# Two groups of value matmuls in one job with one accumulation, and the q score matmuls without a pause, in an attention and MoE kernel

## The chip, the cores and the metric

The kernel runs on one core of one Trainium2 chip. The metric is the device time of one execution in microseconds, as the median of several runs. TensorE (PE) does the matmuls, and its weight loads (PEld) are listed apart; VectorE is DVE, ScalarE is ACT, GpSimd is POOL, and SyncE (SP) issues the DMAs.

## The reference

For each of four batches, 49 agent rows attend to 12480 keys, and 12480 queries attend to the 49 agents; the result goes through a dense layer with the gate `h - tanh(h)`.

```python
def _attn_ref(q, k, v, agents):
    scale = 1.0 / np.sqrt(q.shape[-1])
    def sm(a, b):
        s = scale * (a @ b.transpose(0, 2, 1))
        s = s - s.max(-1, keepdims=True)
        e = np.exp(s)
        return e / (e.sum(-1, keepdims=True) + 1e-09)
    a2k = sm(agents, k)
    agent_v = a2k @ v
    q2a = sm(q, agents)
    return (q2a @ agent_v).astype(np.float32)

def _moe_ref(x, w_in, w_out):
    h = x @ w_in
    g = h - np.tanh(h)
    return (g @ w_out).astype(np.float32)
```

B = 4, N = 12480, C = 128, 49 agents, 2048 hidden units, all float32.

## The kernel before, in words

**The main work.** The 4 x 12480 query rows are cut into 104 blocks of 480 (26 to a batch), and each block has 8 steps of two 128-wide chunks of the hidden layer. `m1` (L441, L442) issues four matmuls of 480 columns into `h`, of which PSUM has three buffers. `act` makes `y` (tanh, L451) and `z` (square, L453) on ACT and `g = h*z` on DVE (L455). POOL copies `g` to `gh` in the rounded format (L485), DVE makes the rest `gl = g - gh` (L490), and `m2` issues six matmuls of 480 columns into the block's accumulator `misc` (L502 and L503 wait for `gh`, L504 for `gl`). The last step of every second block has no split and uses two plain float32 matmuls instead (L500). `finish` takes the accumulator to `o` (L617), and a DMA writes it out. All PSUM tiles named `misc` share two buffers, and the block's accumulator holds one of them from its first `m2` to `finish`.

**The work beside it.** For each pair of blocks `q_softmax` makes the scores of 960 queries (eight float32 matmuls, L396), the maxima, `qe` (POOL, L409) and the probabilities `pp` (POOL, L421); `q_transpose` turns them (L428). While batch b runs its main work, `phase1(b+1)` prepares the agents' attention of the next batch as 34 jobs: 13 `scores` (L238), two for the maximum, 13 `av`, one `sums`, four of `project`, and one empty place. A job is a generator: it goes on by one `yield` in each step of the main loop. Three jobs are started in each pair of blocks, at the steps that `KS` names.

**The value jobs.** The 98 tiles of 128 keys are in 13 groups of 8 (the last has 2). `av(g)` in batches 1 to 3 asks for the load of `v` two groups ahead (four buffers `v0` to `v3`), subtracts the maximum into a tile `ke` on POOL (L276; `ke` has two buffers), takes the exponential on ACT (L278), and issues eight float32 matmuls of 129 columns into a fresh `misc` tile (L292). Tiles of even number write 64 partitions and those of odd number the 49 partitions above them. DVE then copies (first group, L320) or adds (L322) the 113 x 129 result to `acc` in SBUF. Batch 0 has its own first phase, before the main loop, with one accumulation over all groups.

**What sets the order.** The kernel is written step by step, but a scheduler arranges the instructions of each engine when the program is built, so the order on an engine is not that of the code. On the chip each engine then takes its instructions in that fixed order.

Of the kernel before, what the change touches and what calls it, by code (L numbers as in the profile page):

```python
# [11 lines left out]
F32 = mybir.dt.float32  # L12
# [63 lines left out]
class Build:  # L76
# [84 lines left out]
    def phase1(self, b):  # L161
# [108 lines left out]
        def av(g):  # L270
            vt = ahead("v", load_v, g, vb - 1 if b else 1)
            n = tiles(g)
            sv = st["s"][:, g * GT * A : (g * GT + n) * A].rearrange("p (t a) -> p t a", a=A)
            e3 = sv if b == 0 else self.small.tile([128, GT, A], F32, tag="ke", name="ke")[:, :n]
            eng = nc.vector if b == 0 else nc.gpsimd
            eng.tensor_tensor(e3, sv, st["mb"][:, None, :].broadcast_to([128, n, A]), ALU.subtract)  # L276
# [3 lines left out]
            if b == 0:  # L280
                if g == 0:
                    st["ps"] = self.ph.tile([128, 2, 512], F32, tag="h", name="h")[:, 0, :]
                ps, first, last = st["ps"], g == 0, g == NG - 1
            else:
                ps, first, last = self.misc(), True, True
            flat = e3.rearrange("p t a -> p (t a)")
            width = C if b == 0 else C + 1
            for t in range(n):
# [4 lines left out]
                    ps[HALF * odd : HALF * odd + w, :width],  # L293
                    flat[:r, t * A : t * A + w],
                    vt[:r, t, :width],
# [4 lines left out]
            if b == 0:  # L300
                if g == 0:
                    st["es"] = self.small.tile([128, GT * A], F32, tag="ke", name="es")
                elif g < NG - 1:
                    e0 = st["s"][:, : GT * A] if g == 1 else st["es"]
                    nc.vector.tensor_tensor(st["es"], e0, flat, ALU.add)
                if g == NG - 2:
                    st["em"] = self.small.tile([128, A], F32, tag="m", name="es")
                    nc.vector.tensor_reduce(
                        st["em"], st["es"].rearrange("p (t a) -> p a t", a=A), axis=AX.X, op=ALU.add
                    )  # L310
                if g < NG - 1:
                    return
                es = st["em"]
                col = ps[:A, C : C + 1]
                for i, (lhs, r) in enumerate(((es, 128), (e3[:, 0, :], 128), (e3[:, 1, :], TAIL))):
                    nc.tensor.matmul(col, lhs[:r], self.ones[:r, :1], start=(i == 0), stop=(i == 2))
                return
# [422 lines left out]
```

## Time and profile before

| | us |
|---|---|
| median of 3 runs | 2182.68 (2182.53 to 2185.22) |
| profiled execution, its own time | 2180.92 |
| its span | 2179.1 |
| PE busy in the span | 2144.5 (98%) |
| weight loads (PEld) busy | 1799.3 (83%) |
| DVE busy | 2026.2 (93%) |
| ACT busy | 1813.1 (83%) |
| POOL busy | 1395.5 (64%) |

The mean granted TensorE clock of the run is 0.992, and it is 1.00 in all stretches after the first 100 us. A matmul's record is longer than the distance to the next one's start, since matmuls are pipelined; so a pause of PE is seen as idle time only where it is longer than the overlap. The distance between starts shows how fast PE goes. The value jobs of batches 1, 2 and 3 lie in the stretches 296 to 504, 832 to 1041 and 1368 to 1577 us.

### The profile page before, as it was taken

The page shows a single profiled execution, that of the slowest core. Times are in us where ns is not written, and L with a number is a line of the kernel's source. Part 1 is how long each engine was busy: PE and PEld are TensorE (multiplying, and loading weights), DVE is VectorE, ACT ScalarE, POOL GpSimd, SP SyncE. Part 2 cuts the span into 40 slices and gives each one's busy share as a digit, 9 for nine tenths or more (in the row PEclk, how much of TensorE's full clock was granted, in tenths as well). Part 3 has the DMA queues.
Part 4 walks back from the last instruction along what each step waited for, and adds up shares of the span by engine and source line. Part 5 has one row for each costly group of instructions (what it writes and reads, how often), then busy time and mean ns, then how long its engine had stood idle before and what let it go on. Part 6 is the DMA issues. An engine that isn't in the chain of part 4 may idle for free.

```text
span 2179.1 us, 31204 instructions
## 1 busy us (share of the span) xinstructions
PE 2144.5 (98%) x11089; PEld 1799.3 (83%) x11089; DVE 2026.2 (93%) x2120; ACT 1813.1 (83%) x2179; POOL 1395.5 (64%) x933
## 2 busy tenths in 40 slices
PE   7899999999999999999999999999999999999998
PEld 7688878888888887888888888888888888888887
DVE  7898999999999999889999999998999999999998
ACT  4688888888888788888898878888889898989987
POOL 1356567666666556667666556667667677676766
PEclk9799999999999999999999999999999999999999
DMA  9211111110011111111101110121100101010000
GB/s 353 86 58 60 56 38 57 59 57 28 28 48 57 59 48 46 58 59 48 37 19 57 57 50 19 56 65 33 36 20 19 37 19 37 19 37 19 28 10 20
DMA packets 65906, 108.75 MB, mean 50 GB/s; under 512 B 4048, under 2 KB 44240, under 8 KB 65744
## 3 DMA queue, kind: packets, MB, share of 16 engines
q1 hardware_dynamic: 65744, 106.68, 15.2%
q8 instruction: 91, 1.49, 0.3%
q14 instruction: 71, 0.58, 0.1%
HBM read 81.10 MB, written 25.56 MB: 49 GB/s over the span
## 4 chain that ended last, share of the span: by engine, by line
PE 88%; DVE 6%; POOL 3%; issue 2%; ACT 0%; DMA 0%; POOLq 0%; SPq 0%; DVEq 0%; ACTq 0%
PE h L441 15%; PE h L442 15%; PE misc L504 15%; PE misc L502 14%; PE misc L503 14%; PE misc L500 4%; PE misc L396 4%; PE misc L238 3%; POOL gh L485 2%; DVE gl L490 2%; DVE g L455 2%; PE misc L292 2%; PE misc L428 1%; PE h L212 1%; PE misc L370 0%
## 5 line engine op out<-in xcount | busy, mean ns | idle before, releaser
L485 POOL TENSOR_SCALAR gh<-g 128x960 fp32r<-128x960 f32 x780 | 1207.3, 1549 | 665.0 <-DVE g L455 416.5
L490 DVE TENSOR_TENSOR gl<-g,gh 128x960 fp32r<-128x960 f32 x780 | 977.4, 1254 | 89.8 <-PE misc L504 55.7
L455 DVE TENSOR_TENSOR g<-h,z 128x960 f32<-128x960 f32 x832 | 950.5, 1146 | 30.5 <-ACT z L453 27.3
L451 ACT ACTIVATE y<-h 128x960 f32<-128x960 f32 x832 | 802.9, 970 | 186.2 <-PE h L442 182.1
L453 ACT ACTIVATE z<-y 128x960 f32<-128x960 f32 x832 | 832.4, 1007 | 24.3 <-DVE g L455 7.2
L441 PE MATMUL h<-pT,awh 98*128 98x480 f32 x1664 | 662.0, 398 | 1.9 <-DVE awl L374 1.4
L442 PE MATMUL h<-pT,awl 98*128 98x480 f32 x1664 | 631.7, 380 | 0.3 <-DVE awl L374 0.3
L504 PE MATMUL misc<-gl,wo_h 128*128 128x480 f32 x1560 | 607.6, 390 | 3.0 <-DVE gl L490 2.9
L502 PE MATMUL misc<-gh,wo_l 128*128 128x480 f32 x1560 | 601.8, 386 | 4.9 <-POOL gh L485 4.9
L503 PE MATMUL misc<-gh,wo_h 128*128 128x480 f32 x1560 | 593.9, 381 | 0.0
L441 PEld LDWEIGHTS h<-pT,awh 98*128 98x128 f32 x1664 | 313.5, 188 | 65.9 <-issue 13.2
L442 PEld LDWEIGHTS h<-pT,awl 98*128 98x128 f32 x1664 | 315.2, 189 | 57.5 <-issue 10.5
L502 PEld LDWEIGHTS misc<-gh,wo_l 128*128 128x128 f32 x1560 | 294.4, 189 | 59.9 <-POOL gh L485 15.7
L504 PEld LDWEIGHTS misc<-gl,wo_h 128*128 128x128 f32 x1560 | 292.6, 188 | 56.4 <-DVE gl L490 7.9
L503 PEld LDWEIGHTS misc<-gh,wo_h 128*128 128x128 f32 x1560 | 293.3, 188 | 47.1 <-issue 1.2
L409 POOL TENSOR_TENSOR qe<-qe,qm 120x392 f32<-120x392 f32 x52 | 74.2, 1426 | 63.7 <-ACT qe L407 63.7
L396 PEld LDWEIGHTS misc<-ag,qt 128*120 128x120 f32 x832 | 96.3, 186 | 4.0 <-issue 0.3
L617 ACT ACTIVATE o<-misc 128x480 f32<-128x480 f32 x104 | 58.7, 564 | 48.7 <-PE misc L500 33.6
L396 PE MATMUL misc<-ag,qt 128*120 128x49 f32 x832 | 93.6, 265 | 0.0
L500 PE MATMUL misc<-g,wo_f 128*128 128x480 f32 x208 | 92.9, 569 | 0.0
L421 POOL TENSOR_TENSOR pp<-qe,pp 120x392 fp32r<-120x392 f32 x52 | 69.4, 1335 | 36.6 <-ACT pp L419 36.4
L238 PEld LDWEIGHTS misc<-ag,kt 128*128 128x128 f32 x588 | 72.1, 191 | 2.5
(92 smaller groups left out, 864.0 us busy)
## 6 DMA issues: line engine op xcount, KB each, us to landing
qt<-qT SPq DMA_DIRECT2D x52, 480.0 KB, 3.4
outT<-o SPq DMA_DIRECT2D x52, 480.0 KB, 2.6
kt<-kT SPq DMA_DIRECT2D x48, 512.0 KB, 3.6
v<-v SPq DMA_DIRECT2D x36, 512.0 KB, 4.1
vt<-v SPq DMA_DIRECT2D x12, 512.0 KB, 9.4
raw<-w_in SPq DMA_DIRECT2D x4, 512.0 KB, 9.1
raw<-w_out SPq DMA_DIRECT2D x4, 512.0 KB, 8.9
kt<-kT SPq DMA_DIRECT2D x4, 128.0 KB, 2.1
```

What stands on the lines that cost most here:

```text
L396: nc.tensor.matmul(ps[:TT, t * A : (t + 1) * A], qt[:, t * TT : (t + 1) * TT], self.ag[:, b, :], start=True, stop=True)
L441: nc.tensor.matmul(h[:, c, :BLK], aw[0][:A2, sl], pT[:A2], start=True, stop=False)
L442: nc.tensor.matmul(h[:, c, :BLK], aw[1][:A2, sl], pT[:A2], start=False, stop=True)
L451: nc.scalar.activation(y, h[:, :, :BLK], AF.Tanh, scale=TSC)
L453: nc.scalar.activation(z, y.rearrange("p c n -> p (c n)"), AF.Square)
L455: nc.vector.tensor_tensor(self.pair(g), h[:, :, :BLK], self.pair(z), ALU.mult)
L485: self.nc.gpsimd.tensor_scalar(gh, g, 1.0, 0.0, ALU.mult, ALU.add)
L490: self.nc.vector.tensor_tensor(gl, g, gh.bitcast(F32), ALU.subtract)
L500: nc.tensor.matmul(acc[:, :BLK], self.wo_f[:, c, :], gh[:, x], start=first, stop=last)
L502: nc.tensor.matmul(acc[:, :BLK], self.wo_l[:, f, :], gh[:, x], start=first, stop=False)
L503: nc.tensor.matmul(acc[:, :BLK], self.wo_h[:, f, :], gh[:, x], start=False, stop=False)
L504: nc.tensor.matmul(acc[:, :BLK], self.wo_h[:, f, :], gl[:, x], start=False, stop=last)
```

## The change

In batches 1 to 3 the 13 jobs `av(g)` become 7 jobs `av_two(j)`. Such a job asks for the loads of both groups, subtracts for the first group, yields, subtracts for the second, yields, issues both exponentials, yields, and issues up to 16 matmuls into one `misc` tile with one accumulation; then it makes one copy or add. `ke` still has two buffers, and a job fills both. A batch's 34 jobs become 28. In `q_softmax` the eight score matmuls, which had a `yield` after the fourth and after the eighth, are followed by both yields. The value code of batch 0 is the same as before.

```diff
+        def av_two(j):
+            gs = [g for g in (2 * j, 2 * j + 1) if g < NG]
+            vts = [ahead("v", load_v, g, vb - 1) for g in gs]
+            es = []
+            for g in gs:
+                n = tiles(g)
+                sv = st["s"][:, g * GT * A : (g * GT + n) * A].rearrange("p (t a) -> p t a", a=A)
+                e3 = self.small.tile([128, GT, A], F32, tag="ke", name="ke")[:, :n]
+                mb = st["mb"][:, None, :].broadcast_to([128, n, A])
+                nc.gpsimd.tensor_tensor(e3, sv, mb, ALU.subtract)
+                es.append(e3)
+                yield
+            for e3 in es:
+                nc.scalar.activation(e3, e3, AF.Exp, scale=SCALE)
+            yield
+            ps = self.misc()
+            todo = [(g, t, e3, vt) for g, e3, vt in zip(gs, es, vts) for t in range(tiles(g))]
+            for x, (g, t, e3, vt) in enumerate(todo):
...
+                nc.tensor.matmul(
+                    ps[HALF * odd : HALF * odd + w, : C + 1],
...
+                    start=x < 2,
+                    stop=x >= len(todo) - 2,
+                )
+            yield
             acc = st["acc"][: HALF + A]
-            if g == 0:
+            if j == 0:
                 nc.vector.tensor_copy(acc, ps[: HALF + A, : C + 1])
             else:
                 nc.vector.tensor_tensor(acc, acc, ps[: HALF + A, : C + 1], ALU.add)
...
-        jobs += [av(g) for g in range(NG)] + [sums()]
+        jobs += [av(g) for g in range(NG)] if b == 0 else [av_two(j) for j in range(-(-NG // 2))]
+        jobs += [sums()]
...
-            if t % 4 == 3:
-                yield
+        yield
+        yield
```

**The order on PE.** The first value job of batch 1, from the eighth matmul of its first group on; `v0` and `v1` are the groups' values. Before:

```order
L292 MATMUL misc_2908<-v0_87,ke_2875 49x129
L504 MATMUL misc_2742<-gl_2825,wo_h_84 128x480
L502 MATMUL misc_2742<-gh_2797,wo_l_85 128x480
L503 MATMUL misc_2742<-gh_2797,wo_h_84 128x480
L504 MATMUL misc_2742<-gl_2825,wo_h_84 128x480
L502 MATMUL misc_2742<-gh_2823,wo_l_85 128x480
L503 MATMUL misc_2742<-gh_2823,wo_h_84 128x480
L441 MATMUL h_2901<-pT_2759,awh_590 128x480
L442 MATMUL h_2901<-pT_2759,awl_591 128x480
L441 MATMUL h_2901<-pT_2759,awh_590 128x480
L442 MATMUL h_2901<-pT_2759,awl_591 128x480
L504 MATMUL misc_2742<-gl_2847,wo_h_84 128x480
```

And of the change (L331 was L292, L526 was L504, L524 was L502, L525 was L503, L463 and L464 were L441 and L442), from the ninth value matmul on:

```order
L331 MATMUL misc_2931<-v1_88,ke_2886 64x129
L526 MATMUL misc_2742<-gl_2825,wo_h_84 128x480
L524 MATMUL misc_2742<-gh_2797,wo_l_85 128x480
L525 MATMUL misc_2742<-gh_2797,wo_h_84 128x480
L526 MATMUL misc_2742<-gl_2825,wo_h_84 128x480
L524 MATMUL misc_2742<-gh_2823,wo_l_85 128x480
L525 MATMUL misc_2742<-gh_2823,wo_h_84 128x480
L463 MATMUL h_2902<-pT_2759,awh_590 128x480
L464 MATMUL h_2902<-pT_2759,awl_591 128x480
L463 MATMUL h_2902<-pT_2759,awh_590 128x480
L464 MATMUL h_2902<-pT_2759,awl_591 128x480
L331 MATMUL misc_2931<-v1_88,ke_2886 49x129
```

The second group's matmuls follow at once, but not in one run: the first job's 16 stand as runs of 9, 4, 1 and 2 with matmuls of the main work between them. The value matmuls of a batch stood in runs of 8, 8, 8, 7, 1, 8, 8, 8, 8, 8, 7, 1, 8, 8, 2 and now stand in runs of 9, 4, 1, 2, 10, 1, 5, 16, 4, 12, 9, 4, 3, 16, 2: 15 runs to a batch both times. The eight score matmuls of a pair (L396) stand in one run in all pairs but the first, before as after.

**The order on POOL.** In the middle of batch 1's value jobs, beginning with a `gh` copy; `ke` is the subtraction of a value job, `pp` that of the query softmax. Before:

```order
L485 TENSOR_SCALAR gh_3258<-g_3256 128x960
L276 TENSOR_TENSOR ke_3412<-s_740,mb_2663 128x392
L485 TENSOR_SCALAR gh_3307<-g_3305 128x960
L485 TENSOR_SCALAR gh_3337<-g_3335 128x960
L421 TENSOR_TENSOR pp_3320<-qe_3226,pp_3320 120x8x49
L276 TENSOR_TENSOR ke_3569<-s_740,mb_2663 128x392
L485 TENSOR_SCALAR gh_3358<-g_3356 128x960
L485 TENSOR_SCALAR gh_3380<-g_3378 128x960
L485 TENSOR_SCALAR gh_3401<-g_3399 128x960
L276 TENSOR_TENSOR ke_3704<-s_740,mb_2663 128x392
```

And of the change (L507 was L485, L319 was L276, L443 was L421):

```order
L507 TENSOR_SCALAR gh_3294<-g_3292 128x960
L319 TENSOR_TENSOR ke_3326<-s_744,mb_2663 128x392
L319 TENSOR_TENSOR ke_3337<-s_744,mb_2663 128x392
L443 TENSOR_TENSOR pp_3358<-qe_3261,pp_3358 120x8x49
L507 TENSOR_SCALAR gh_3345<-g_3343 128x960
L319 TENSOR_TENSOR ke_3461<-s_744,mb_2663 128x392
L507 TENSOR_SCALAR gh_3368<-g_3366 128x960
L319 TENSOR_TENSOR ke_3468<-s_744,mb_2663 128x392
L507 TENSOR_SCALAR gh_3405<-g_3403 128x960
L507 TENSOR_SCALAR gh_3428<-g_3426 128x960
```

The four subtractions of two jobs and a `pp` now stand beside three `gh` copies, where two or three copies stood between one subtraction and the next. The same piece stands in each of batches 1, 2 and 3. Ahead of a batch's value jobs (but for one score matmul in the first step of the main loop) and from the next batch's first score job on, PE's order is the same as before.

## Rows read from the trace of the kernel before

**Rows 1.** The page: busy time of each engine, and the chain that ended last.

```profile
PE 2144.5 (98%) x11089; PEld 1799.3 (83%) x11089; DVE 2026.2 (93%) x2120; ACT 1813.1 (83%) x2179; POOL 1395.5 (64%) x933
PE 88%; DVE 6%; POOL 3%; issue 2%; ACT 0%; DMA 0%; POOLq 0%; SPq 0%; DVEq 0%; ACTq 0%
```

**Rows 2.** Windows: length, busy us (instructions) of PE, PEld, DVE, ACT, POOL, clock, DMA, GB/s.

```profile
296.00:504.00 208.00, 207.74 (x1125) 171.05 (x1123) 190.92 (x202) 174.89 (x210) 143.94 (x98) 1.00 0.18 55
832.00:1041.00 209.00, 208.76 (x1132) 172.05 (x1131) 192.46 (x203) 175.02 (x210) 144.86 (x98) 1.00 0.18 55
1368.00:1577.00 209.00, 208.77 (x1131) 172.03 (x1130) 192.54 (x203) 175.44 (x211) 143.60 (x98) 1.00 0.14 45
1650.00:2150.00 500.00, 500.00 (x2417) 423.21 (x2416) 481.98 (x479) 449.39 (x519) 359.63 (x227) 1.00 0.08 25
```

**Rows 3.** Timeline of PE about one value job of eight matmuls: start, us, what.

```profile
471.41 0.38 PE L442 MATMUL h<-pT,awl 98*128 98x480 f32 x1
471.72 1.09 PE L292 MATMUL misc<-v,ke 128*64 128x129 f32 x16
472.75 0.48 PE L504 MATMUL misc<-gl,wo_h 128*128 128x480 f32 x1
473.07 0.38 PE L502 MATMUL misc<-gh,wo_l 128*128 128x480 f32 x1
473.29 0.38 PE L503 MATMUL misc<-gh,wo_h 128*128 128x480 f32 x1
```

**Rows 4.** Timeline of PE about a run of one value matmul.

```profile
435.14 0.37 PE L504 MATMUL misc<-gl,wo_h 128*128 128x480 f32 x1
435.44 0.42 PE L292 MATMUL misc<-v,ke 128*49 128x129 f32 x2
435.80 1.07 PE L500 MATMUL misc<-g,wo_f 128*128 128x480 f32 x2
```

**Rows 5.** Chain that ended last, two of its pieces in the last batch.

```profile
1956.80 1.62 PE misc L396 x16
...
1968.08 1.61 PE misc L500 x4
```

**Rows 6.** Groups by line: shapes xcount | busy us, mean ns | idle before, releasers.

```profile
L485 POOL TENSOR_SCALAR gh<-g 128x960 fp32r<-128x960 f32 x780 | 1207.3, 1549 | 665.0 <-DVE g L455 416.5 <-PE misc L503 72.3 <-DVE qs L415 65.0
...
L455 DVE TENSOR_TENSOR g<-h,z 128x960 f32<-128x960 f32 x832 | 950.5, 1146 | 30.5 <-ACT z L453 27.3
L453 ACT ACTIVATE z<-y 128x960 f32<-128x960 f32 x832 | 832.4, 1007 | 24.3 <-DVE g L455 7.2
L451 ACT ACTIVATE y<-h 128x960 f32<-128x960 f32 x832 | 802.9, 970 | 186.2 <-PE h L442 182.1
...
L421 POOL TENSOR_TENSOR pp<-qe,pp 120x392 fp32r<-120x392 f32 x52 | 69.4, 1335 | 36.6 <-ACT pp L419 36.4
...
L276 POOL TENSOR_TENSOR ke<-s,mb 128x392 f32<-128x392 f32 (+1 forms) x39 | 48.2, 1240 | 9.5 <-PE misc L292 9.5
...
L322 DVE TENSOR_TENSOR acc<-acc,misc 113x129 f32<-113x129 f32 x36 | 10.1, 280 | 3.0 <-PE misc L292 3.0
```

**Rows 7.** Timeline of POOL where batch 1's first two subtractions stand together.

```profile
282.10 2.80 POOL L276 TENSOR_TENSOR ke<-s,mb 128x392 f32<-128x392 f32 x2
284.87 1.96 POOL L485 TENSOR_SCALAR gh<-g 128x960 fp32r<-128x960 f32 x2
289.08 1.74 POOL L485 TENSOR_SCALAR gh<-g 128x960 fp32r<-128x960 f32 x1 [2.25 <-PE misc L504]
```

**Rows 8.** Timeline of PE in the same stretch, the rows with a wait.

```profile
285.92 0.48 PE L502 MATMUL misc<-gh,wo_l 128*128 128x480 f32 x1 [0.65 <-POOL gh L485]
287.89 0.48 PE L504 MATMUL misc<-gl,wo_h 128*128 128x480 f32 x1 [0.39 <-DVE gl L490]
290.87 0.48 PE L502 MATMUL misc<-gh,wo_l 128*128 128x480 f32 x1 [0.53 <-POOL gh L485]
```

**Rows 9.** The page's DMA issues: what, queue, count, KB each, us to landing.

```profile
v<-v SPq DMA_DIRECT2D x36, 512.0 KB, 4.1
```

More of the change, by code (lines that the diff above doesn't have):

```diff
@@ L270, in av @@
         def av(g):
-            vt = ahead("v", load_v, g, vb - 1 if b else 1)
+            vt = ahead("v", load_v, g, 1)
             n = tiles(g)
[L273 to L276, printed above, removed]
+            e3 = st["s"][:, g * GT * A : (g * GT + n) * A].rearrange("p (t a) -> p t a", a=A)
+            nc.vector.tensor_tensor(e3, e3, st["mb"][:, None, :].broadcast_to([128, n, A]), ALU.subtract)
             yield
@@ L279, in av @@
             yield
-            if b == 0:
-                if g == 0:
[L282 to L285, printed above, removed]
+            if g == 0:
+                st["ps"] = self.ph.tile([128, 2, 512], F32, tag="h", name="h")[:, 0, :]
+            ps, first, last = st["ps"], g == 0, g == NG - 1
             flat = e3.rearrange("p t a -> p (t a)")
-            width = C if b == 0 else C + 1
             for t in range(n):
@@ L292, in av @@
                 nc.tensor.matmul(
-                    ps[HALF * odd : HALF * odd + w, :width],
+                    ps[HALF * odd : HALF * odd + w, :C],
                     flat[:r, t * A : t * A + w],
-                    vt[:r, t, :width],
+                    vt[:r, t, :C],
                     start=(first and t < 2),
@@ L299, in av @@
             yield
[L300 to L316, printed above, removed]
-                return
+            if g == 0:
+                st["es"] = self.small.tile([128, GT * A], F32, tag="ke", name="es")
+            elif g < NG - 1:
+                e0 = st["s"][:, : GT * A] if g == 1 else st["es"]
+                nc.vector.tensor_tensor(st["es"], e0, flat, ALU.add)
@@ new lines, in av @@
+            if g == NG - 2:
+                st["em"] = self.small.tile([128, A], F32, tag="m", name="es")
+                nc.vector.tensor_reduce(
+                    st["em"], st["es"].rearrange("p (t a) -> p a t", a=A), axis=AX.X, op=ALU.add
+                )
+            if g < NG - 1:
+                return
+            col = ps[:A, C : C + 1]
+            for i, (lhs, r) in enumerate(((st["em"], 128), (e3[:, 0, :], 128), (e3[:, 1, :], TAIL))):
+                nc.tensor.matmul(col, lhs[:r], self.ones[:r, :1], start=(i == 0), stop=(i == 2))
@@ new lines, in av_two @@
+        def av_two(j):
[16 more added lines that the diff above has]
+            for x, (g, t, e3, vt) in enumerate(todo):
+                r = rows(g, t)
+                odd = t % 2
+                w = A if odd else HALF
+                nc.tensor.matmul(
+                    ps[HALF * odd : HALF * odd + w, : C + 1],
+                    e3.rearrange("p t a -> p (t a)")[:r, t * A : t * A + w],
+                    vt[:r, t, : C + 1],
+                    start=x < 2,
+                    stop=x >= len(todo) - 2,
+                )
+            yield
@@ L318, in av @@
             acc = st["acc"][: HALF + A]
-            if g == 0:
+            if j == 0:
                 nc.vector.tensor_copy(acc, ps[: HALF + A, : C + 1])
```

## The prediction, made before the changed kernel ran

> **What bounds the kernel now.** I read the page first. PE is busy for 98% of the span and carries 88% of the chain that ended last; DVE is busy for 93% and the weight loads for 83% [rows 1]. The reader is to see that two engines are near the limit, so the averages alone don't tell which of them sets the time. The windows do. In the three stretches with value jobs PE is idle for 208 - 207.74 = 0.26, 209 - 208.76 = 0.24 and 209 - 208.77 = 0.23 us, and in the last 500 us for nothing, while DVE has 16 to 18 us to spare in each [rows 2]. So PE is the bound there, and the pauses that a change could remove are 0.73 us in all, plus what is hidden under PE's overlapping records. Next I read the timeline for PE's pace: two 480-column matmuls start 0.22 us apart (473.07 to 473.29) [rows 3]. The kernel's time is then the sum of what PE issues, plus the places where it stands still, and I cost the change by these two.
>
> **What the value matmuls cost PE.** Eight of them in one run: from the start of the matmul before (471.41) to that of the second one behind (473.07) are 1.66 us, where the two ordinary distances are 0.44; the run costs 1.22 us [rows 3]. The distance just behind the first is 472.75 to 473.07, or 0.32 and not 0.22, so 0.10 of this falls after the run. A run of one costs 435.80 - 435.14 - 0.22 = 0.44 us [rows 4], and with the same 0.10 behind it 0.54. I take it that matmuls go in pairs of even and odd tiles (they write different partitions) and that a lone one costs as much as a pair. Then three more pairs cost 1.22 - 0.54 = 0.68, or about 0.22 a pair, and a run has a fixed part of 0.54 - 0.22 = 0.32 to 1.22 - 4 x 0.22 = 0.34 us; I use 0.34.
>
> **What the change does to that sum.** In the built order a batch has 15 runs before and 15 now, so the fixed parts stay: 45 x 0.34 us both times. A run of odd length fills its last pair by half. Before, a batch's runs hold 51 pairs, now 52 (9, 4, 1, 2 are 5 + 2 + 1 + 1, and so on). This adds 3 x 0.22 = **+0.66 us**. Merging the jobs therefore brings PE nothing, since the scheduler cut the 16 into pieces.
>
> **The score matmuls.** They stood in one run already: the chain shows all 16 of their records (two to a float32 matmul) as one piece of 1.62 us [rows 5]. In the built order this holds before and after for every pair but the first. The cost is **0**.
>
> **The adds.** 18 of the 36 adds on DVE go: 18 x 0.280 = 5.0 us of DVE time [rows 6]. In the value stretches DVE has 16 us to spare each and PE hardly waits [rows 2], so I count **0** on the path. If DVE were the bound, it would be the whole 5.0 (a rival, below).
>
> **The exponentials, the subtractions and the loads** stay in number. The loads of `v` are asked for two at a time; they land in a median of 4.1 us [rows 9], and a group is used one job, about five steps of ten 0.22-us matmuls or 11 us, after its load was asked for. What waits behind such a load on SP's queue is a query load or an output, and the 11 us cover these too: **0**. Without that cover a late load would hold PE for up to 4.1 us.
>
> **The subtractions' places on POOL.** This is the term that no row prices. `ke` has two buffers, and a job now fills both, so the next job's subtraction waits on POOL until PE is through with the value matmuls that read the buffer; the `gh` copies are queued behind it, and PE's L502 waits for these. I bound it at the densest place, the piece of POOL's order in the section on the change. In the built order, between PE's first use of `gh_3345` and that of `gh_3405` PE has 20 ordinary matmuls and four short transposes (about 0.3 us): 20 x 0.22 + 0.3 = 4.7 us. POOL has two subtractions and two copies to do in that time. Two subtractions in a row took 2.80, two copies in a row 1.96, one copy beside DVE work 1.74 us [rows 7]. At best this is 2.80 + 1.96 = 4.8 us, just PE's pace. At worst every subtraction is as long as the longer of the two must have been (2.80 - 0.98 = 1.82, with a copy's 0.98 for the other) and every copy 1.74: 2 x 1.82 + 2 x 1.74 = 7.1 us, 2.4 too long. Against this stands what POOL has in hand when the piece begins. From the end of `h_3328` (the tile from which `gh_3345` is made) to the first use of `gh_3345` PE has 22 matmuls (4.8), the plain pair (1.61 [rows 5]), a run of 4 (0.34 + 0.44) and one of 12 (0.34 + 1.32): 8.9 us. The chain it needs is y 0.97, z 1.01, g 1.15 and gh 1.55 [rows 6], 4.7 us; two subtractions and `pp` (2.80 + 1.34) ahead of the copy would fill the rest if none of it overlapped, and most does, since they need not wait for `h_3328`. So the cost is between 0 and 2.4 us a batch. A gain is no end of it, because PE's idle time in a whole value stretch is 0.26 us at most. I take 0.5, nearer to the lower end as the best case just fits and the slack at the start is real: **+1.5 us** for three batches, with ends of -0.7 (every present pause gone) and +7.2.
>
> **The sum.** 0.66 + 0 + 0 + 0 + 1.5 = +2.2 us on the profiled execution's own 2180.92 us, which is 1.8 below the median of the runs shown; I put it on that median: 2182.7 + 2.2 = **2184.9 us**. A difference of 0.2%, 4.4 us, is about what a measurement of this kernel can tell from no change, so I forecast no change.
>
> **Rivals.**
> - *Slower: the second subtraction holds POOL's queue.* The trace has one place where two subtractions stand together, at the start of each batch's value jobs; there two copies come behind them and PE waits 0.65 + 0.39 + 0.53 = 1.57 us [rows 7, 8]. The change keeps that place and makes a denser one. If it costs the upper end, 2.4 us in each of three batches, the time is 2182.7 + 0.7 + 7.2 = 2190.6. It decides against my forecast from (4.4 - 0.7) / 3 = 1.2 us a batch on. Against it: at the place in the trace no value matmuls gave PE other work, and here 16 lie ahead. A sentence apart: the Trainium skill, SBUF — State Buffer, Who interferes with whom, says that a DVE instruction with two SBUF inputs contends with a GpSimd one that reads SBUF; the copies' 0.98 alone and 1.74 beside DVE [rows 7] agree, and by it the lengths near the worst case are the likely ones wherever `gl` runs beside. Chance 0.20.
> - *Slower: the accumulator waits for the tile.* A value tile is now open over up to four steps, and the next block's accumulator needs its buffer. Each late opening would cost what may stand ahead of the add on DVE, one 1.15-us operation [rows 6], and the add's 0.28: 1.4 us, once a batch, +4.3 with the 0.7: 2187.7. In the built order two `m1` (1.8 us) stand between the first tile's last matmul and that opening, which covers it. Chance 0.05.
> - *Faster: DVE is the bound after all.* DVE is busy for 482 of the last 500 us [rows 2]. If every removed add counted, the time would be 2182.7 - 5.0 = 2177.7. Against it: the adds lie where DVE has room, and their rows name no PE that waits. The Trainium skill's Perfetto Trace Analysis, Identifying the Most-Contended Engine, would judge PE by its weight loads and not by its matmul rows; by that, PE's 83% is under DVE's 93% [rows 1] and this rival is what follows. The pace of 0.22 us without a pause speaks against it here. Chance 0.07.
> - *Faster: the change does what its words say,* and the 16 go through PE in one run. Seven runs a batch instead of 15 save 24 x 0.34 = 8.2, and 49 pairs instead of 51 save 6 x 0.22 = 1.3: 2173.2 us. The built order excludes it, unless the fixed part belongs to the job and not to the run; the run of one that costs 0.54 speaks against that. Chance 0.02.
>
> **How the numbers follow.** My forecast has 0.66. Faster by over 0.2%: 0.07 + 0.02 = 0.09. Slower by over 0.2%: 0.20 + 0.05 = 0.25. Within: 0.66. The range goes from 2178.0, at the edge of the DVE rival, to 2191.0, just over the upper end of the POOL rival; it leaves out about a tenth. The forecast's own range is 2181 to 2187.
>
> **What would show it.** Right: 15 runs of L331 a batch at 0.34 us plus 0.22 a pair, 18 adds of 0.28 us, PE idle for under 1.5 us in each value stretch, and DVE's busy time lower by 5 us with the span unchanged. The POOL rival: L524 waits for `gh` at the middle of the value jobs in every batch, with a subtraction of 1.8 us or a wait for PE just ahead on POOL. The DVE rival: the stretch ends earlier by as much as DVE lost. Wrong in another way: value runs whose cost doesn't follow the pairs, or pauses of PE outside the value stretches.

## The result: slower by 0.17%, within the forecast, one reason of it wrong

The changed kernel takes **2187.93 us** (median of 22 runs, 2182.51 to 2190.89), the kernel before 2184.32 beside it (22 runs, 2180.41 to 2186.46). The ratio is 1.0017, 95% interval 1.0011 to 1.0024: 2.4 to 5.2 us more. The forecast was 2184.9 us, the range 2178.0 to 2191.0.

The page of the changed kernel, busy time and chain (lines behind the value jobs stand 22 lower than before: the `gh` copy is L507, the matmul that waits for it L524; the value matmuls are L331):

```profile
PE 2149.4 (98%) x11089; PEld 1803.5 (82%) x11089; DVE 2024.7 (93%) x2102; ACT 1810.3 (83%) x2179; POOL 1384.6 (63%) x933
PE 89%; DVE 6%; POOL 3%; issue 2%; ACT 0%; DMA 0%; POOLq 0%; SPq 0%; DVEq 0%; ACTq 0%
```

PE's share of the chain is 89% instead of 88% [rows 1], DVE has 18 instructions fewer, and PE is still the bound. DVE's busy time fell by 1.5 us only and not by the 5 of the adds, since its `gl` operations took 3 us longer in all (977.4 before, 980.5 now). The windows of the three value stretches and of the end are those of [rows 2], each moved along with its stretch:

```profile
300.00:508.00 208.00, 207.18 (x1103) 168.54 (x1102) 190.67 (x200) 172.04 (x209) 135.71 (x96) 1.00 0.18 53
837.00:1046.00 209.00, 208.16 (x1107) 169.44 (x1106) 191.60 (x201) 173.04 (x210) 136.69 (x97) 1.00 0.17 53
1374.00:1583.00 209.00, 208.19 (x1108) 169.48 (x1107) 191.70 (x202) 172.96 (x211) 137.61 (x97) 1.00 0.14 43
1657.00:2157.00 500.00, 500.00 (x2417) 423.47 (x2416) 482.27 (x479) 448.94 (x518) 358.75 (x227) 1.00 0.07 25
```

PE is now idle for 0.81 to 0.84 us in each stretch instead of 0.23 to 0.26; the last 500 us are as they were.

**Where the profiled difference lies.** The profiled executions differ by 7.4 us (spans 2179.1 and 2186.5), twice the medians' 3.6. I set the end of each output piece on ScalarE against the same piece of before. 4.29 us are there by 270 us, before the first value job of the change; then 0.93, 1.47 and 0.80 us come in the three batches, and nothing elsewhere. (Of these, 0.16 to 0.25 us a batch come behind the last value job, where the jobs that follow stand at other places; in batch 1 that is 559 to 680 us.) So the change costs 3.2 us, and the 4.29 are no part of it. They go with the granted clock in the first 90 us. Two windows of before, then the same two of the change:

```profile
57.00:70.00 13.00, 9.85 (x24) 4.86 (x23) 10.47 (x24) 3.37 (x8) 0.00 (x0) 0.50 0.57 180
...
73.00:87.00 14.00, 12.75 (x58) 10.27 (x59) 12.37 (x14) 9.21 (x13) 7.17 (x6) 0.83 0.12 36
```

```profile
57.00:70.00 13.00, 10.12 (x25) 5.11 (x25) 10.16 (x25) 2.99 (x7) 0.00 (x0) 0.51 0.58 186
...
73.00:87.00 14.00, 12.37 (x37) 9.81 (x38) 9.61 (x12) 6.06 (x8) 5.79 (x4) 0.51 0.01 1
```

The figure behind POOL's count is the granted clock. In 73 to 87 us the change ran at half speed (0.51, the level of 1.2 GHz) and PE has 37 records, before ran at 0.83 and has 58. Across the profiles below the difference that stands at 270 us is -0.9 to +5.8 us, in no order that goes with the edits. All later readings are therefore steps between two outputs, not differences of spans: "start" is what stood at 270 us, "batch" what each batch's value jobs added to the profile of before.

**The value runs.** A whole job of 16 in one run, and a run of three, in PE's timeline (start, us, what):

```profile
351.00 0.38 PE L525 MATMUL misc<-gh,wo_h 128*128 128x480 f32 x1
351.31 1.98 PE L331 MATMUL misc<-v,ke 128*64 128x129 f32 x32
353.22 0.48 PE L526 MATMUL misc<-gl,wo_h 128*128 128x480 f32 x1
353.54 0.38 PE L524 MATMUL misc<-gh,wo_l 128*128 128x480 f32 x1
...
374.54 0.38 PE L526 MATMUL misc<-gl,wo_h 128*128 128x480 f32 x1
374.85 0.64 PE L331 MATMUL misc<-v,ke 128*49 128x129 f32 x6
375.42 0.48 PE L463 MATMUL h<-pT,awh 98*128 98x480 f32 x1
375.75 0.38 PE L464 MATMUL h<-pT,awl 98*128 98x480 f32 x1
```

Read as in [rows 3], from the start ahead to the start of the second behind, less two ordinary distances, the 16 cost 353.54 - 351.00 - 0.44 = 2.10 us and the three 375.75 - 374.54 - 0.44 = 0.77. By 0.34 a run and 0.22 a pair it would be 2.10 and 0.78. All runs of a batch together cost 16.93 us before and 16.99 now; 0.18 of each run that stands beside the plain pair belongs to that pair (two runs before, one now), which leaves 16.57 and 16.81. The batch's last run, of two matmuls, does not follow the prices: it costs 0.91 us and not 0.56, before as now.

**The score matmuls, the adds and the rest.** In the chain that ended last, the 16 score records are one piece as in [rows 5]; the adds are 18 at the old length [rows 6]; POOL's subtractions have the old length and more idle time ahead of them (14.1 us instead of 9.5):

```profile
391.50 1.62 PE misc L418 x16
```

```profile
L507 POOL TENSOR_SCALAR gh<-g 128x960 fp32r<-128x960 f32 x780 | 1189.1, 1526 | 669.3 <-DVE g L477 444.4 <-PE misc L525 77.4 <-PE misc L526 44.9
...
L319 POOL TENSOR_TENSOR ke<-s,mb 128x392 f32<-128x392 f32 (+1 forms) x39 | 48.2, 1242 | 14.1 <-PE misc L331 6.6 <-ACT y L473 5.3 <-ACT z L475 1.4
L343 DVE TENSOR_TENSOR acc<-acc,misc 113x129 f32<-113x129 f32 x18 | 5.0, 277 | 0.0
```

**The waits.** In batch 1 PE waits three times in the middle of the value jobs, for `gh`: 0.48 us at 385.23, 0.15 at 426.59, 0.19 at 467.19. Before, it waited 0.26 at 331.38 and 0.24 at 537.37. Batches 2 and 3 repeat this. By the distances of the starts (a record hides part of a wait) the three are 1.30 us too long, the two of before 0.82: +0.48 (with the 0.10 us that each also leaves behind it, as in [rows 3], it is +0.58). The longest, on PE and on POOL:

```profile
383.17 0.48 PE L524 MATMUL misc<-gh,wo_l 128*128 128x480 f32 x1
...
385.23 0.48 PE L524 MATMUL misc<-gh,wo_l 128*128 128x480 f32 x1 [0.48 <-POOL gh L507]
```

```profile
372.58 0.95 POOL L319 TENSOR_TENSOR ke<-s,mb 128x392 f32<-128x392 f32 x1 [1.76 <-ACT y L473]
373.50 1.96 POOL L507 TENSOR_SCALAR gh<-g 128x960 fp32r<-128x960 f32 x2
375.64 1.63 POOL L319 TENSOR_TENSOR ke<-s,mb 128x392 f32<-128x392 f32 x1 [0.19 <-PE misc L331]
377.25 1.90 POOL L507 TENSOR_SCALAR gh<-g 128x960 fp32r<-128x960 f32 x1
382.12 3.06 POOL L507 TENSOR_SCALAR gh<-g 128x960 fp32r<-128x960 f32 x2 [2.96 <-PE misc L525]
```

A subtraction that waited for value matmuls (375.64) does stand ahead. But POOL is idle for 2.96 us between the copy behind it and the two copies that PE waits for. The row puts the end of this down to PE's L525. That is only the matmul that ended last: in the built order (as e_ke4_fixed below writes it out) it reads the tile copied at 377.25, and the last reader of the buffer that the copy at 382.12 fills is the L525 that started at 379.02. What the copy starts with is its own `g`: 606 of this trace's 780 copies start 0.15 to 0.19 us after their `g` has ended on DVE, and so do these two. PE, DVE and the second copy there:

```profile
379.23 0.38 PE L526 MATMUL misc<-gl,wo_h 128*128 128x480 f32 x1
```

```profile
379.70 1.16 DVE L512 TENSOR_TENSOR gl<-g,gh 128x960 fp32r<-128x960 f32 x1 [1.41 <-POOL gh L507]
380.78 2.22 DVE L477 TENSOR_TENSOR g<-h,z 128x960 f32<-128x960 f32 x2
383.15 1.16 DVE L512 TENSOR_TENSOR gl<-g,gh 128x960 fp32r<-128x960 f32 x1 [0.15 <-POOL gh L507]
```

```profile
383.18 2.00 POOL L507 TENSOR_SCALAR gh<-g 128x960 fp32r<-128x960 f32 x1
```

DVE takes a `gl` and the two `g` back to back. The `gl` needs the copy that ended at 379.16 and one of two `gl` buffers, and by the built order the last reader of its buffer is the L526 at 379.23. It starts 0.09 us after that matmul has ended, and in batches 2 and 3 it is the same (0.09 us behind the L526 that ended at 917.32 and at 1454.50). So the wait goes back to PE itself, which reads a `gl` tile late, over three operations on DVE, to the copies. The second copy then takes 2.00 us and the first 1.00, as DVE's next `gl` began 0.03 us ahead of the second (last section). That speaks against the subtraction already; the experiments decide it.

### The profile page after: what moved, and what is told of

Its sections match the earlier page's. It is cut to its first block, busy times and chain, and to the rows that moved or that the text cites. A ratio compares the mean times of both kernels' runs of the same rounds, so it can differ in the third digit from the quotient of the medians.

```text
span 2186.5 us, 31233 instructions
## 1 busy us (share of the span) xinstructions
PE 2149.4 (98%) x11089; PEld 1803.5 (82%) x11089; DVE 2024.7 (93%) x2102; ACT 1810.3 (83%) x2179; POOL 1384.6 (63%) x933
## 4 chain that ended last, share of the span: by engine, by line
PE 89%; DVE 6%; POOL 3%; issue 2%; ACT 0%; DMA 0%; POOLq 0%; SPq 0%; DVEq 0%; ACTq 0%
PE h L463 15%; PE h L464 15%; PE misc L526 15%; PE misc L524 15%; PE misc L525 14%; PE misc L418 4%; PE misc L522 4%; PE misc L238 3%; POOL gh L507 2%; DVE g L477 2%; PE misc L331 2%; DVE gl L512 2%; PE misc L450 1%; PE h L212 1%; PE misc L392 0%
## 5 line engine op out<-in xcount | busy, mean ns | idle before, releaser
L507 POOL TENSOR_SCALAR gh<-g 128x960 fp32r<-128x960 f32 x780 | 1189.1, 1526 | 669.3 <-DVE g L477 444.4
L512 DVE TENSOR_TENSOR gl<-g,gh 128x960 fp32r<-128x960 f32 x780 | 980.5, 1258 | 96.8 <-PE misc L526 49.5
L463 PE MATMUL h<-pT,awh 98*128 98x480 f32 x1664 | 660.2, 397 | 1.9 <-DVE awl L396 1.4
L464 PE MATMUL h<-pT,awl 98*128 98x480 f32 x1664 | 632.2, 380 | 0.3 <-DVE awl L396 0.3
L526 PE MATMUL misc<-gl,wo_h 128*128 128x480 f32 x1560 | 609.8, 391 | 3.2 <-DVE gl L512 3.1
L524 PE MATMUL misc<-gh,wo_l 128*128 128x480 f32 x1560 | 604.4, 387 | 6.0 <-POOL gh L507 5.7
L525 PE MATMUL misc<-gh,wo_h 128*128 128x480 f32 x1560 | 595.0, 381 | 0.0
L463 PEld LDWEIGHTS h<-pT,awh 98*128 98x128 f32 x1664 | 313.7, 188 | 65.3 <-issue 11.5
L464 PEld LDWEIGHTS h<-pT,awl 98*128 98x128 f32 x1664 | 315.2, 189 | 56.1 <-issue 9.2
L524 PEld LDWEIGHTS misc<-gh,wo_l 128*128 128x128 f32 x1560 | 295.2, 189 | 62.5 <-POOL gh L507 18.0
L526 PEld LDWEIGHTS misc<-gl,wo_h 128*128 128x128 f32 x1560 | 293.4, 188 | 57.4 <-DVE gl L512 8.5
L525 PEld LDWEIGHTS misc<-gh,wo_h 128*128 128x128 f32 x1560 | 294.0, 188 | 47.4 <-issue 1.8
L443 POOL TENSOR_TENSOR pp<-qe,pp 120x392 fp32r<-120x392 f32 x52 | 75.5, 1452 | 40.3 <-ACT pp L441 39.8
```

Source lines behind the costliest of these rows:

```text
L463: nc.tensor.matmul(h[:, c, :BLK], aw[0][:A2, sl], pT[:A2], start=True, stop=False)
L464: nc.tensor.matmul(h[:, c, :BLK], aw[1][:A2, sl], pT[:A2], start=False, stop=True)
L507: self.nc.gpsimd.tensor_scalar(gh, g, 1.0, 0.0, ALU.mult, ALU.add)
L512: self.nc.vector.tensor_tensor(gl, g, gh.bitcast(F32), ALU.subtract)
L524: nc.tensor.matmul(acc[:, :BLK], self.wo_l[:, f, :], gh[:, x], start=first, stop=False)
L525: nc.tensor.matmul(acc[:, :BLK], self.wo_h[:, f, :], gh[:, x], start=False, stop=False)
```

## Experiments

| kernel | us (runs) | ratio to before, 95% | start | batch 1, 2, 3 |
|---|---|---|---|---|
| the change | 2187.93 (22) | 1.0017 (1.0011 to 1.0024) | +4.3 | +0.9, +1.5, +0.8 |
| e_q_alone | 2184.62 (11) | 1.0000 (0.9990 to 1.0010) | +1.7 | -0.1, -0.1, -0.2 |
| e_adds_back | 2187.10 (11) | 1.0006 (0.9996 to 1.0016) | +4.3 | +0.6, +1.1, +0.4 |
| e_one_run | 2197.28 (5) | 1.0064 (1.0050 to 1.0078) | +0.2 | +4.8, +5.0, +4.6 |
| e_ke4 | 2184.86 (11) | 1.0003 (0.9994 to 1.0012) | +2.1 | -0.2, 0.0, +0.2 |
| e_ke4_fixed | 2189.95 (8) | 1.0027 (1.0014 to 1.0039) | +0.2 | +2.0, +1.9, +1.8 |
| e_before_ke4 | 2188.80 (8) | 1.0025 (1.0015 to 1.0036) | +1.9 | +1.9, +1.8, +2.1 |
| e_short_subtract | 2181.35 (10) | 0.9985 (0.9975 to 0.9994) | +4.5 | -1.2, -0.8, -1.4 |
| e_even_first | 2212.32 (4) | 1.0126 (1.0112 to 1.0141) | +5.8 | +8.8, +8.8, +8.6 |
| e_few_runs_ke4 | 2200.58 (6) | 1.0077 (1.0062 to 1.0091) | -0.1 | +7.0, +7.5, +5.3 |
| e_light_run_ke4 | 2195.35 (4) | 1.0046 (1.0031 to 1.0061) | +5.2 | +2.3, +4.4, +2.8 |
| e_before_even | 2179.35 (12) | 0.9984 (0.9975 to 0.9993) | +0.2 | -0.9, -0.8, -0.9 |
| e_ke4_even | 2179.74 (12) | 0.9991 (0.9981 to 1.0000) | -0.9 | -1.2, +0.2, -1.4 |

The kernel before has medians of 2184.2 to 2184.8 beside these. "Start" and "batch" are us against its profile.

**One part of the change alone (e_q_alone).** Only the `yield`s are moved; the value jobs are those of before.

```diff
- if t % 4 == 3:
-     yield
+ yield
+ yield
```

> The kernel before, with the score matmuls' two yields behind the eighth matmul and nothing else changed. Theory (they stood in one run already): the value stretches are as long as before to 0.1 us each, and the time is the same. Rival, the early yield had kept PE from a wait: PE's waits for gh come at other places, and a pair of blocks is longer by 0.1 us or more, 5 us in all.

No batch moves by more than 0.2 us. The score matmuls' part of the change does nothing.

**The adds given back (e_adds_back).**

```diff
+ nc.vector.tensor_tensor(acc, acc, acc, ALU.max)
```

> The change, with a second DVE operation of the add's size behind each of its 18 adds (the maximum of the sum with itself, which changes nothing), so DVE has its 5 us back; the order on PE and POOL is the same. Theory (DVE has room in the value stretches): the time stays within 1 us of the change. Rival, DVE is the bound: 18 x 0.28 = 5 us slower than the change.

The batches cost no more than in the change (PE's order differs from the change's in a few places). DVE is not the bound, and the 5.0 us taken from it were worth nothing.

**What a run and a pair cost (e_even_first).**

```diff
- todo = [(g, t, e3, vt) for g, e3, vt in zip(gs, es, vts) for t in range(tiles(g))]
+ todo = [(g, t, e3, vt) for o in (0, 1) for g, e3, vt in zip(gs, es, vts) for t in range(o, tiles(g), 2)]
```

> The change, with the 16 matmuls of a job in another order: first the eight of the even tiles, then the eight of the odd ones, so that neighbours write the same partitions. Theory (an even and an odd matmul go together, and a lone one costs as much as a pair): of the 52 pairs a batch only those at the border of the two halves are left, and up to 98 - 52 = 46 prices of 0.22 us are added a batch: 10 us a batch at most, 20 to 30 us in all, about 2208 to 2218 us, and a run of 16 takes about 3.5 to 3.9 us instead of 2.0. Rival (a matmul of 129 columns costs its own share, 0.11 to 0.12 us, whatever its neighbour): no more than 2 us from the change, and a run of 16 still takes 2.0 us.

The same 16 matmuls in PE's timeline of this kernel:

```profile
353.74 0.37 PE L464 MATMUL h<-pT,awl 98*128 98x480 f32 x1
354.04 3.34 PE L331 MATMUL misc<-v,ke 128*64 128x129 f32 x32
357.31 0.48 PE L526 MATMUL misc<-gl,wo_h 128*128 128x480 f32 x1
357.63 0.38 PE L524 MATMUL misc<-gh,wo_l 128*128 128x480 f32 x1
```

They cost 357.63 - 353.74 - 0.44 = 3.45 us instead of 2.10, and a batch 25.6 instead of 17.0. An even and an odd matmul do go together; one without its partner takes a pair's time. The run of 16 keeps one pair, at the border of its halves: 0.34 + 15 x 0.22 = 3.64; the measured 0.2 less was not followed.

**All 16 in one run (e_one_run).** The change, with an order on PE alone:

```diff
+ for i in pe[max(0, n0 - NEAR) : n0]:
+     self.tc.add_manual_dep(pe[n0], i.name, info, reason="run of values")
+ for i in pe[n1 + 1 : n1 + 1 + NEAR]:
+     self.tc.add_manual_dep(i, last, info, reason="run of values")
```

> The change, with each job's 16 value matmuls held together on PE by an ordering rule alone (no wait is added): 7 runs of value matmuls a batch instead of 15, 49 pairs instead of 52. Theory (a run has a fixed part of 0.34 us and a pair costs 0.22): 24 x 0.34 + 9 x 0.22 = 10.1 us less than the change, so about 6 to 7 us less than the kernel before, unless gh or gl come later. Rival, the fixed part belongs to the job or the matmul and not to the run: within 2 us of the change. Rival, a long run starves DVE and ACT: PE waits for gh behind the runs, and 3 or more of the 10 us come back.

A miss by 20 us. The runs do what their price says: 13.87 us a batch instead of 16.99. But a batch takes 4.8 us more than before, so by difference some 8 us of waits came with them; 3.7 us of these are idle time in PE's rows from 300 to 520 us, six waits for `gl` above all. PE in that kernel:

```profile
323.63 0.38 PE L530 MATMUL misc<-gh,wo_h 128*128 128x480 f32 x1
324.50 0.48 PE L531 MATMUL misc<-gl,wo_h 128*128 128x480 f32 x1 [0.49 <-DVE gl L517]
...
325.57 1.97 PE L333 MATMUL misc<-v,ke 128*64 128x129 f32 x32
```

PE stands still for `gl` with 32 records of ready value work directly behind. The cuts of the planner's order are what it pays to fill such waits, and 0.34 us a cut is cheap beside a wait of 0.65 (0.87 from start to start).

**Softer forms of the same order (e_light_run_ke4, e_few_runs_ke4).** With four `ke` buffers, and with 6 instructions ahead and 6 behind tied (light), or 4 and 24 (few), instead of 24 and 24; of the light form:

```diff
- for i in pe[max(0, n0 - NEAR) : n0]:
+ for i in pe[max(0, n0 - 6) : n0]:
...
- for i in pe[n1 + 1 : n1 + 1 + NEAR]:
+ for i in pe[n1 + 1 : n1 + 1 + 6]:
```

> The change with four buffers of ke and the order rule tied to 6 instructions before and 6 behind each run: seven runs and 49 pairs a batch, as in the kernel with the rule over 24 instructions, which took about 13 us more than before. By the prices of runs and pairs alone 9.5 us less than before, about 2174 us. Theory (the rule puts each run behind the last matmul of the step before, which waits for gl, and takes from the scheduler the matmuls that filled that wait): 8 to 12 waits for gl of about 0.5 us in the records (0.65 by the distances) a batch stay, and the time is 2188 to 2197 us. Rival (what cost time was that the rule reached over 24 instructions): waits for gl mostly gone, 2174 to 2180 us.

> The change with four buffers of ke and an order rule on TensorE that ties a run of value matmuls to the 4 instructions before it and the 24 behind it: 11 runs and 51 pairs a batch, where before has 15 and 51 and the change with four buffers 12 and 52. Theory (a run has a fixed price of 0.34 us, a pair 0.22): 3 x 0.56 = 1.7 us less than the change with four buffers, 3 x 4 x 0.34 = 4.1 less than before plus what the buffers give, so about 2179 to 2181 us. Rival (what a long run saves comes back as waits for gl, because the pieces were what filled these waits): each of the four removed cuts leaves a wait of about 0.5 to 0.65 us, and the time is 2184 us or more, with waits of TensorE for gl behind the runs.

Neither made a long run cheaper, and neither time has the reason that was expected. In the light form the time is in the theory's range, but between 300 and 520 us PE waits only twice for `gl` (0.8 us in all, where 8 to 12 waits were expected), 0.6 us for `gh` and once 1.4 us ahead of a value run. The other form missed its forecast by 20 us: PE waits 3.4 us ahead of two value runs and 1.5 us for `g`. The first of these two:

```profile
341.96 1.78 PE L423 MATMUL misc<-ag,qt 128*120 128x49 f32 x16
345.46 1.75 PE L333 MATMUL misc<-v,ke 128*64 128x129 f32 x28 [1.72 <-ACT qe L434]
```

All these waits stand ahead of the first matmul of a run of 16 and end with ScalarE's copy of the query scores out of their `misc` tile (L434). A job's 16 matmuls need a `misc` tile of their own, there are two, and the accumulator holds one: a job that may not be cut waits until the scores are out of the other. In both forms the granted clock also falls after long waits of PE, at six places in the second (0.57 in 357 to 361 us).

**Four buffers of `ke` (e_ke4, e_before_ke4, e_ke4_fixed).**

```diff
- e3 = self.small.tile([128, GT, A], F32, tag="ke", name="ke")[:, :n]
+ e3 = self.small.tile([128, GT, A], F32, tag="ke", name="ke", bufs=4)[:, :n]
```

> The change, with four buffers for the subtracted scores instead of two, so that POOL's subtraction need not wait for PE to be through with the job before. The built order differs: 12 runs a batch and 52 pairs. Theory (runs at 0.34 us, and subtractions that hold the gh copies): 9 runs less are 3.1 us, and PE's three waits for gh in each value stretch (0.82 us a batch in the change) become shorter, by up to 2.5 us in all: 3 to 5 us less than the change. Rival, the waits come from the density on POOL and not from the buffer: only the 3.1 us, and the waits for gh stay.

3.1 us less than the change, which the theory and the rival both allow. The waits for `gh` in the middle fell from 0.82 to 0.47 us, and it looked like proof that the two buffers had been the cost. Two controls took that back. The first is the same edit on the kernel before:

> The kernel before, with four buffers of ke instead of two, and nothing else: value runs on TensorE as before (15 a batch, 51 pairs). Theory (the two buffers hold POOL's queue already in the kernel before, but only where two subtractions stand together, at the start of each batch's value jobs, where TensorE waits 1.57 us): that wait falls to about 0.4 us as it did in the change with four buffers, the small waits of 0.26 and 0.24 us stay or go; 1.2 to 1.7 us a batch less, 3.5 to 5 us less than before in all. Rival (buffers matter only in the change's denser pieces): within 1 us of before, and the 1.57 us stays. If the four buffers gain as much here as they gained on the change (about 3 us), what they took from the change was not the change's own cost, and the added 0.9 us a batch has to be told by the waits in the middle of the value jobs instead.

There the four buffers *cost* 1.9 us a batch: neither theory. The wait at the maximum did not fall to 0.4 us in either kernel, as this expectation has it of e_ke4: it is 1.34 for `gh` and 0.40 for `gl` in e_ke4, 1.33 and 0.38 here. The built order differs from that of before on all four engines, so the edit also moved the order. So the second control writes the change's order out on four engines, by a dependency without a semaphore from each instruction to the next, and gives it the four buffers:

```diff
+ for steps in json.loads(zlib.decompress(base64.b64decode(ORDER))).values():
+     names = [f"I-{n}" for n in accumulate(steps) if f"I-{n}" in here]
+     for a, b in zip(names, names[1:]):
+         self.tc.add_manual_dep(here[b], a, info, reason="order of the change")
```

> The change with four buffers of ke, and the order of the instructions on TensorE, GpSimd, DVE and ScalarE written out as the change has it (so the planner moves nothing: 15 value runs, 52 pairs a batch). Only the waits of POOL for a buffer can change. Theory (both buffers held: POOL's subtraction waits for TensorE's value matmuls, and the gh copies stand behind it): the three waits of TensorE for gh in the middle of the value jobs, 0.82 us a batch in the change's records, fall under 0.4, and a batch takes 0.4 to 1.0 us less than in the change: about 1.2 to 3 us less in all. Rival (POOL's queue is simply too long there, two subtractions and two copies against TensorE's pace): the three waits stay at 0.8 us, and the time is that of the change within 1 us. Second rival (four buffers helped the change because the planner then chose another order): likewise the change's time.

The three waits stay, at 0.45, 0.13 and 0.20 us. POOL in this kernel ahead of the first:

```profile
372.55 1.97 POOL L367 TENSOR_TENSOR ke<-s,mb 128x392 f32<-128x392 f32 x1
374.49 1.90 POOL L555 TENSOR_SCALAR gh<-g 128x960 fp32r<-128x960 f32 x1
378.83 3.04 POOL L555 TENSOR_SCALAR gh<-g 128x960 fp32r<-128x960 f32 x2 [2.44 <-PE misc L574]
```

The subtraction no longer waits for PE, starts earlier, takes 1.97 us instead of 1.63, and the first copy of the pair again starts 0.18 us after its `g`. The held buffers are not the cause, and freeing them made a batch 0.5 to 1.0 us longer than in the change. PE's order is the same in both, so the starts can be set side by side: 0.84 us are lost from 366 to 379 us, of which 0.13 at the first `h` matmuls, 0.48 at a wait for `gl` (0.20 us of idle time at 377.64) and 0.18 at the `h` matmuls just behind it. That `gl` waited for the copy at 374.49, which the longer subtraction held for 1.85 us. What e_ke4 had gained is in its order: 12 runs instead of 15, and value runs of 15.82 us a batch instead of 16.99.

**The subtraction cut short (e_short_subtract), in the change's own order.**

```diff
- nc.gpsimd.tensor_tensor(e3, sv, mb, ALU.subtract)
+ nc.gpsimd.tensor_tensor(e3[:, :1], sv[:, :1], mb[:, :1], ALU.subtract)
...
- nc.scalar.activation(e3, e3, AF.Exp, scale=SCALE)
+ nc.scalar.activation(e3, sv, AF.Exp, scale=SCALE)
```

> The change with the change's own order written out, and POOL's subtraction cut to the first of a group's eight tiles (49 of 392 columns); the exponential then reads the scores themselves, so the maximum is left out of the values. All buffers, waits for buffers and orders stay; POOL has about 13 x 0.8 = 10 us less work a batch. Theory (POOL's queue, by waits for buffers or by length, is what delays gh): if it is mostly length, the waits of TensorE for gh in the middle go (under 0.2 of 0.82 us), and those at the maximum too (1.57 us before), and the kernel is 2 to 7 us faster than the change. If it is mostly the held buffers, the waits in the middle stay near 0.8 and only those at the maximum go. Rival (gh is late for a cause outside POOL, such as g on DVE): the waits stay everywhere.

The waits at the maximum fall from 1.57 us [rows 8] to 0.25. Those in the middle stay at 0.48, 0.07 and 0.18. PE and POOL at the first:

```profile
383.36 0.48 PE L573 MATMUL misc<-gh,wo_l 128*128 128x480 f32 x1 [0.48 <-POOL gh L556]
```

```profile
373.78 0.30 POOL L367 TENSOR_TENSOR ke<-s,mb 128x49 f32<-128x49 f32 x1 [0.85 <-PE misc L380]
374.05 2.00 POOL L556 TENSOR_SCALAR gh<-g 128x960 fp32r<-128x960 f32 x1
380.25 3.06 POOL L556 TENSOR_SCALAR gh<-g 128x960 fp32r<-128x960 f32 x2 [4.19 <-PE misc L574]
```

With subtractions of 0.30 us POOL is idle for 4.19 us and PE still waits 0.48. In the middle it is the expectation's rival that holds: `gh` is late because `g` on DVE is. Both copies again start 0.18 us after their `g`, and DVE's three operations stand ahead of them as in the change ("issue": the profile names no releaser):

```profile
377.84 1.16 DVE L561 TENSOR_TENSOR gl<-g,gh 128x960 fp32r<-128x960 f32 x1 [2.64 <-issue]
378.92 2.21 DVE L526 TENSOR_TENSOR g<-h,z 128x960 f32<-128x960 f32 x2
```

The copy that this `gl` needs had ended at 376.06; the last PE reader of its buffer ended at 377.74, 0.10 us ahead of it. So of POOL's subtractions neither the buffers nor the length makes the change's wait. What is left is the order on PE: it reads a `gl` tile late, which holds DVE, and then asks for two new copies 2.06 us apart, while two take 3.06. That the two `gl` buffers do it is read from the built order and the times; a third was not tried.

**The order made cheaper (e_before_even, e_ke4_even).** Each kernel's own order written out, with single value matmuls moved across a cut so that runs are even: in before the lone one joins the seven ahead of it (13 runs, 49 pairs), in e_ke4 four move (10 runs, 49 pairs). The runs of a batch, first of before and then of e_ke4:

```diff
- 8, 8, 8, 7, 1, 8, 8, 8, 8, 8, 7, 1, 8, 8, 2
+ 8, 8, 8, 8, 8, 8, 8, 8, 8, 8, 8, 8, 2
...
- 9, 5, 2, 9, 6, 1, 16, 16, 15, 1, 16, 2
+ 10, 4, 2, 10, 6, 16, 16, 16, 16, 2
```

> The kernel before with its own order written out on TensorE, GpSimd, DVE and ScalarE, with one move: the lone value matmul behind each run of seven joins that run (13 runs and 49 pairs a batch instead of 15 and 51). By the prices of 0.34 us a run and 0.22 a pair: 2 x 0.34 + 2 x 0.22 = 1.1 us a batch, 3.4 us in all less than before. Rival (the lone matmul filled a wait, as the runs in the kernels with the order rule did): the gain comes back as a wait of TensorE where it stood, and the time is that of before within 1 us, or slower.

> The change with four buffers of ke and that kernel's own order written out, with the value matmuls at the borders of the runs moved so that every run has an even length (10, 4, 2, 10, 6, 16, 16, 16, 16, 2: 10 runs and 49 pairs instead of 12 and 52). By the prices: 2 x 0.34 + 3 x 0.22 = 1.3 us a batch, 4.0 us in all less than the change with four buffers, so about 3 us less than before: 2181 us. Rival (the moved matmuls filled waits): no better than the change with four buffers.

In e_before_even each of the two moves takes 0.53 to 0.56 us off the next output, which is 0.34 + 0.22, and 0.26 to 0.32 comes back once a batch: the lone run had covered part of a wait.

```profile
372.69 0.37 PE L492 MATMUL h<-pT,awl 98*128 98x480 f32 x1
373.12 0.48 PE L552 MATMUL misc<-gh,wo_l 128*128 128x480 f32 x1
```

0.43 from start to start there, 0.21 over the ordinary distance. The kernel is faster than before by 0.07 to 0.25% (5.3 us by the medians, 2.5 by the batches' steps, 3.4 expected), and faster than the change. e_ke4_even, the change's own form with two more buffers, ends at 0.9991 (0.9981 to 1.0000). Its value runs cost 14.52 us a batch against 15.82 in e_ke4, the 1.3 that the prices gave, and its batches take 2.6 us in all off those of e_ke4, of 4.0 expected. The rest came back at the maximum of batch 2, by the clock (windows as in [rows 2]):

```profile
819.00:824.00 5.00, 3.25 (x14) 1.89 (x13) 3.59 (x4) 4.89 (x8) 5.00 (x6) 1.00 0.02 3
824.00:828.00 4.00, 4.00 (x12) 3.31 (x13) 3.89 (x4) 1.74 (x2) 0.68 (x1) 0.57 0.00 0
```

PE had stood idle for 1.33 and 0.40 us just before; then the granted clock is 0.57 in 4 us, matmuls start 0.40 instead of 0.22 us apart, and 1.26 us are lost against the same matmuls of e_ke4. So the merged job can be had without its loss, but merging is not what gains: the kernel before with two matmuls moved is as fast.

## Why the prediction was right, and where it was not

- **"What the value matmuls cost PE": right.** Over runs of 1, 4, 8, 10 and 16 the two prices give 0.56, 0.78, 1.22, 1.44 and 2.10 us; measured 0.55, 0.78, 1.22, 1.44 and 2.10. Even tiles first (within 0.2 us), and one matmul moved, gave the same prices; the last run of two does not follow them (0.91 for 0.56), but is the same before and after. The Trainium skill's TensorEngine Tiling (Array Packing), Key Properties, says that tiles of the array work independently of each other and that a change of the tiling mode drains TensorE; it gives no time. Both agree with the rows: a lone matmul takes a pair's 0.22 us, and 0.34 us go with each change between these matmuls and the others.
- **"Merging the jobs brings PE nothing": right,** 0.24 us more a batch without the plain pairs' share, 0.22 forecast. The rival "all 16 in one run" had its saving right too (9.5 us in all; 3 x (16.93 - 13.87) = 9.2 measured), and would not have been faster: its price is the waits that the pieces had filled, which no step of mine counted.
- **The score matmuls at 0 and the adds at 0: right,** each shown alone. The rival "DVE is the bound after all" falls, and with it the verdict by weight loads, one of the two measures that the Trainium skill's Perfetto Trace Analysis, Identifying the Most-Contended Engine, names for TensorE: 83% of PE's loads stood under 93% of DVE, and 18 operations more on DVE cost nothing here. One sign failed: DVE's busy time fell by 1.5 us, not 5.
- **"The subtractions' places on POOL": the size right, the mechanism wrong.** I took 0.5 us a batch, and the waits for `gh` in the middle grew by 0.48. But the step said that the next job's subtraction waits for a buffer of `ke` and that the `gh` copies queue behind it. With that wait gone, in the same order, the waits stayed; with the subtraction cut to 0.30 us, likewise. So the 0.5 us was right by luck. I had compared POOL's work with PE's between two uses of `gh`, and not asked when `g` is made and when PE gives a `gl` buffer back. A row of before already showed that DVE's idle time before `gl` ends mostly with PE's reader of `gl`:

```profile
L490 DVE TENSOR_TENSOR gl<-g,gh 128x960 fp32r<-128x960 f32 x780 | 977.4, 1254 | 89.8 <-PE misc L504 55.7 <-POOL gh L485 29.8 <-POOL qe L409 1.6
```

The step also took the copies' 0.98 us [rows 7] for copies alone. The second of those two lay beside a `gl` that began after it, and it was the `gl` that grew, to 1.93 us. The rival "the second subtraction holds POOL's queue" showed its sign, L524 waiting for `gh` in every batch with a subtraction that waited for PE ahead, but at 0.48 us and by another cause; no wait for the accumulator's tile is in the trace.

- **What stays open.** Of 0.9, 1.5 and 0.8 us a batch, 0.24 are pairs and 0.48 waits for `gh`. In batch 2 another 0.56 comes just ahead of the maximum: PE's wait for `gl` is 0.46 us instead of 0.21 there, and a matmul for `gl` at 808.33 starts 0.37 us after the one before it instead of 0.21, which with 0.09 behind it makes 0.25 more. The last 0.1 to 0.2 us of each batch I could not place.

The sum was 0.66 + 1.5 = +2.2; the batches' steps give +3.2, the medians +3.6 (2.4 to 5.2). The forecast of no change larger than 0.2% held, narrowly.

## What to carry to other kernels

When a planner sets the order, price an edit from the built order: count the runs and the matmuls without a partner, and ask of each piece which wait it fills before you join it to another. When an edit of a buffer or an operation also moves the order, its time says nothing of the mechanism; write the old order out and make the edit again. A wait for a copy has two ends: see what the copying engine itself waited for, and what that waited for in turn, since a buffer that the waiting engine gives back late, even one on a third engine, looks like a slow copy. And do not take the releaser that a row names on trust: it is the one that came last, and only the built order says whether it touched the same buffer.

## What was not expected of the hardware

The granted clock in the first 90 us differs from one execution to the next: 0.83 or 0.51 in the same 14 us, and the two profiles above stand 4.3 us apart behind it, more than the change itself. With one profile of each kernel the whole difference would have been read as 7.4 us. The clock also fell for a few microseconds in mid-run, at some of the places where PE had waited 1.3 to 1.7 us (0.57 in the row above), in five of the six kernels with four `ke` buffers. In the other kernels, where PE's longest wait after the first 100 us was 0.65 us, it did so only at the very end. GpSimd's work takes longer beside one operation of DVE, `gl`. In the trace of the change the 526 `gh` copies that begin while a `gl` runs take 1.75 us (the `gl` 1.15), the 115 that begin before a `gl` 1.00 (that `gl` then 1.82), and the 139 without one 1.00, all medians. Beside `g` a copy keeps its 1.00 us. The subtraction's 0.95 to 1.97 us in the rows above are the same thing: 0.95 beside `g`, 1.63 and 1.97 beside `gl`. That is what the prediction has beside its first rival, and here it decides how long the second of two copies takes.
